# Low halves of the prepared inputs on VectorE in place of GpSimd, with the scale folded in

## The chip, the core and the metric

The kernel runs on one core of a Trainium2 chip. A core has five engines that run side by side, each through its own instructions in a fixed order: TensorE (PE in the profile; its weight loads are PEld), VectorE (DVE), ScalarE (ACT), GpSimd (POOL) and SyncE (SP), which here only issues DMAs. An instruction waits for semaphores that others raise, and whatever is queued behind it on its engine waits too. The metric is device time of one execution in microseconds (us), lower is better. TensorE is granted one of two clocks, 1.2 or 2.4 GHz; the profile gives the granted clock as a share of the higher.

## What is computed

A recurrent attention layer (batch 4, 8 heads, 768 steps, head size 40), and two feed-forward layers on its output (3072 tokens, width 320, inner width 2048):

```python
for t in range(S):
    y[:, :, t] = np.einsum('bhd,bhde->bhe', rt, state)
    Sa = np.einsum('bhde,bhe->bhd', state, at)
    state_decay = state * wt[:, :, None, :] - np.einsum('bhd,bhe->bhde', Sa, bt)
    state = state_decay + np.einsum('bhd,bhe->bhde', vt, kt)
...
h = x @ w_in
g = h * (1.0 / (1.0 + np.exp(-h)))      # second layer: g = h - np.tanh(h)
return (g @ w_out).astype(np.float32)
```

## The kernel before

The 768 steps are cut into 12 chunks of 64 (c = 0 to 11). A chunk's inputs come in two halves of 16 heads (hf = 0 and 1), so there are 24 preparations; below they are counted n = 2c + hf, and "even" means hf = 0.

Float32 products are made of float16 matmuls: a value x is held as a high half, float16 of x, and a low half, float16 of x minus the high half, each multiplied apart. `prep(c, hf)` makes these halves. It takes four loaded tiles: `w` (decays), `ra` (a), `rkb` (k and b, 768 columns) and `rrv` (receptances r and values v, 384 columns each). VectorE scans the decays forward (L224) and backward (L230), scales a (L229) and k, b (L233). ScalarE rounds to float16 (L234 for k and b, L235 for a, L237 for r, L238 for v). GpSimd first multiplies r and v by 1024 in place (`pscale`, called on L236, shown under L193), and then makes the low halves: of k and b on L239 (on VectorE in chunk 0), of a, v and r by `psub`, which all stand under L190. High and low halves go to a tile `HL`, of which there is one, and from there twelve DMAs per preparation (L250) spread them over a tile `LR` (five buffers), which the matmuls read. While those DMAs read HL, the next preparation can't write it.

From LR, `p1` (L270, tile p1a) makes a chunk's 64x64 products, evicted by `p1e` (L278 mK on VectorE, L282 and L283 bP on ScalarE). `sol_in` transposes them (L305), and `sol_step` solves a triangular system on VectorE in 31 dependent steps of two instructions (L314 tmp, L316 Tl), which the other work of VectorE is put in between. `sol_out` transposes back (L326, L327). Merges (`mg`) and the chain `ch_x`, `ch_u`, `ch_s`, `ch_y`, `ch_m` follow on TensorE with evictions on ScalarE and VectorE; the state for the next chunk goes through `Md` (VectorE, L440), `MT` (ScalarE, L447) and its low half `lows` (GpSimd, L190). The first feed-forward layer (`hp` L569, `o` L591 to L593, with `gl` L579 on VectorE) runs on TensorE among this, about a chunk and a half behind. In the first 600 us all weights are also split into halves: `conv_f32` (L525 to L528 on ScalarE and VectorE), low halves by `psub` on GpSimd (tiles wih, woh, w2s). The second feed-forward layer runs alone after 862 us; there GpSimd makes only `gl`.

The order is not written by hand. Each task has a planned time from a table (`SC`); sorted by it they go to a scheduler, which places every instruction by a cost model of its own. A change of engine or length in `prep` so moves the order on all engines. `psub` and `pscale` are one line each: a `tensor_tensor` subtract and a `tensor_scalar` multiply on GpSimd.

Of the kernel before, what the change touches and what calls it, by code (L numbers as in the profile page):

```python
# [12 lines left out]
AF = mybir.ActivationFunctionType  # L13
ALU = mybir.AluOpType
# [4 lines left out]
C = 64  # L19
# [12 lines left out]
S_R = 2.0 ** 10  # L32
S_V = S_R
# [14 lines left out]
def _poly():  # L48
# [37 lines left out]
    x=(-0.9631, -0.0175, 2.3021, 1.3623),  # L86
# [20 lines left out]
def build(tc, pk, tv, w1i, w1o, w2i, w2o, out, nch=NCH, dbg=None):  # L107
    nc = tc.nc
    PE, ACT, DVE, POOL, SP = nc.tensor, nc.scalar, nc.vector, nc.gpsimd, nc.sync
# [67 lines left out]
    def planes(HL):  # L177
        return [HL[:, :, o:o + n] for o, n in ((0, LW), (LW, 2 * C), (RW, LW), (RW + LW, 2 * C))]
# [10 lines left out]
    def psub(out, a, b):  # L189
        POOL.tensor_tensor(out, a, b, ALU.subtract)  # L190

    def pscale(out, a, sc):
        POOL.tensor_scalar(out, a, sc, 0.0, ALU.mult, ALU.add)  # L193
# [16 lines left out]
    def prep(c, hf):  # L210
        w, ra, rkb, rrv = raw_t.pop((c, hf))
        hl = HL
        if c == 0 and hf == 1:
            hl = lr_slot().rearrange("p u n -> p (u n)")[0:120, 0:12 * RW].rearrange("p (j n) -> p j n", j=6)
            DVE.memset(planes(hl)[0][:, :, 3 * C:LW], 0.0)
        ll, rh, lh, rl = planes(hl)
        k0, v0 = (0, 2 * C) if c % 2 == 0 else (C, 0)

        av, kb, rv, vv = [x.rearrange("p (j t) -> p j t", j=6) for x in (ra, rkb, rrv[:, 0:384], rrv[:, 384:768])]

        pt = at_p.tile([120, 392], F32, tag="pq", name="pq", bufs=1)
        pr = at_p.tile([120, 392], F32, tag="pr", name="pr", bufs=1)
        pq = pt[:, 0:390].rearrange("p (j t) -> p j t", t=65)
        DVE.tensor_tensor_scan(pt[:, 0:390], w[:, 0:390], d1a.rearrange("p j t -> p (j t)"), 0.0, ALU.mult, ALU.add)  # L224
        DVE.reciprocal(out=d1b[:, 65:391:65], in_=pt[:, 64:390:65])
        DVE.tensor_scalar(lh[:, :, 3 * C:3 * C + 1], pq[:, :, C:C + 1], S_P * S_KB / P_INIT, None, ALU.mult)
        DVE.scalar_tensor_tensor(out=lh[:, :, 3 * C + 1:LW], in0=pq[:, :, C:C + 1], scalar=S_P * S_KB / P_INIT,
                                 in1=lh[:, :, 3 * C:3 * C + 1], op0=ALU.mult, op1=ALU.subtract)
        DVE.scalar_tensor_tensor(out=av, in0=av, scalar=-S_A * S_KB, in1=pq[:, :, 0:C], op0=ALU.mult, op1=ALU.mult)  # L229
        DVE.tensor_tensor_scan(pr[:, 2:391][:, ::-1], w[:, 2:391][:, ::-1], d1b[:, 2:391][:, ::-1], 0.0, ALU.mult, ALU.add)  # L230
        pi = pr[:, 2:392].rearrange("p (j t) -> p j t", t=65)[:, :, 0:C]
        kbv = kb.rearrange("p j (q t) -> p j q t", q=2)
        DVE.tensor_tensor(kbv, kbv, pi.unsqueeze(2).to_broadcast([120, 6, 2, C]), ALU.mult)  # L233
        ACT.activation(out=lh[:, :, k0:k0 + 2 * C], in_=kb, func=AF.Copy)  # L234
        ACT.activation(out=rh[:, :, 0:C], in_=av, func=AF.Copy)  # L235
        pscale(rrv, rrv, S_R)  # L236
        ACT.activation(out=rh[:, :, C:2 * C], in_=rv, func=AF.Copy)  # L237
        ACT.activation(out=lh[:, :, v0:v0 + C], in_=vv, func=AF.Copy)  # L238
        (DVE if c == 0 else POOL).tensor_tensor(ll[:, :, k0:k0 + 2 * C], kb, lh[:, :, k0:k0 + 2 * C], ALU.subtract)  # L239
        psub(rl[:, :, 0:C], av, rh[:, :, 0:C])  # L240
        psub(ll[:, :, v0:v0 + C], vv, lh[:, :, v0:v0 + C])
        psub(rl[:, :, C:2 * C], rv, rh[:, :, C:2 * C])
        if c == 0:
            gates["pool"] = nc.cur_bb.bb.instructions[-1]
        LR = lr_slot()
        for i in range(3):
            n = 6 if i < 2 else 4
            src, dst = hl[i * 40:i * 40 + 40, 0:n], LR[:, 6 * i:6 * i + n]
            for pl, s0, d0, w in ((0, RW, 0, LW), (0, LW, LW, 2 * C), (1, RW, 0, RW), (2, 0, 0, RW)):
                SP.dma_start(out=dst[pl * 40:pl * 40 + 40, :, d0:d0 + w], in_=src[:, :, s0:s0 + w])  # L250
        LR = LR[0:120].rearrange("p (u j) n -> p u j n", u=2)
        L, R = LR[:, :, :, 0:LW], LR[:, :, :, LW:RW]
        if c == 0:
            gates["sp"] = nc.cur_bb.bb.instructions[-1]

        for i, j0, n, u in ((0, 0, 6, 0), (1, 0, 2, 0), (1, 2, 4, 1), (2, 0, 4, 1)):
            h = 6 * i + j0 - 8 * u
            SP.dma_start(out=pd[c, hf, 40 * h:40 * (h + n), u].rearrange("(h d) t -> d h t", d=40),
                         in_=pq[40 * i:40 * i + 40, j0:j0 + n, 0:C])
        p63 = at_p.tile([40, 2, 8, 1], F32, tag="p63", name="p63", bufs=5)  # L260
        POOL.tensor_tensor(p63, L[0:40, :, :, 3 * C:3 * C + 1], L[0:40, :, :, 3 * C + 1:LW], ALU.add)
        L_t[c, hf], R_t[c, hf], P_t[c, hf] = L, R, p63
# [36 lines left out]
    def lr_slot():  # L299
        return at_p.tile([128, 16, RW], F16, tag="LR", name="LR", bufs=5)  # L300
# [356 lines left out]
    for c in range(nch):  # L657
        T0 = 8.0 * c
        T1 = T0 + (SC["d"][c] if c < len(SC["d"]) else 0)
        for hf in range(2):  # L660
            when(T1 + SC["raw"][hf], load_raw, c, hf, after=[("prep", c - 1 + hf, 1 - hf)] if c else [])
            when(T1 + SC["prep"][hf], prep, c, hf, after=[("load_raw", c, hf)] + ([("prep", c, 0)] if hf else []))
            when(T0 + SC["v"][hf], load_v, c, hf, after=[("ch_y", c - 1, 2 * hf), ("ch_y", c - 1, 2 * hf + 1)])
# [123 lines left out]
```

## Time and profile before

| | before |
|---|---|
| runs | 1231.36, 1231.57, 1233.86 us, median 1231.57 |
| profiled execution, its own time | 1226.61 us |
| its span, first to last instruction | 1224.9 us |
| mean granted TensorE clock | 0.951 |
| busy: PE, DVE, ACT, POOL | 85%, 77%, 67%, 33% of the span |

A busy share is a mean over stages: up to about 100 us TensorE has little to do, from 120 to 745 us attention, the first layer and the preparations run together, from 745 to 862 us the first layer finishes, and then the second runs alone. Rows of the trace name an engine, a line, the tiles written and read, the count, the busy time and the mean duration, and for waits what ended them. TensorE's waits are read as time lost, since its work stands in a fixed order and its backlog is there to be done.

### The profile page before, as it was taken

To read this page: it belongs to the slowest core of one execution; us is meant where nothing else is said; L and a number is where in the kernel's file an instruction comes from. 1 tells how busy PE (TensorE), PEld (TensorE's weight loads), DVE (VectorE), ACT (ScalarE), POOL (GpSimd) and SP (SyncE) were. 2 spreads that over 40 slices of the span, in tenths; PEclk is the share of its full clock that TensorE was granted. 3 is DMA by queue.
4 is the path that set the end of the run, shared out by engine and by line. 5 is a ranking of instruction groups with operands and counts; after the bars stand their busy time and mean duration, and the time that the engine had idled before them with its cause. 6 is when DMAs were issued, how large, how long until landed. Compare 5 with 4: busy or idle time off the path is not lost.

```text
span 1224.9 us, 32035 instructions
## 1 busy us (share of the span) xinstructions
PE 1035.7 (85%) x12624; PEld 861.4 (70%) x12624; DVE 943.0 (77%) x1847; ACT 819.7 (67%) x1586; POOL 402.9 (33%) x488
## 2 busy tenths in 40 slices
PE   0006659888989998988999999999899999999997
PEld 0006547777767777777778778888778888888885
DVE  6788899788877988888868887723367888888885
ACT  2468678756666576666655655544468888888885
POOL 5345352433323442343242321010033333333332
PEclk9998659989997999899999999999999999999998
DMA  6676655465645555464434332111711111111000
GB/s 161 180 195 180 176 157 148 142 160 139 162 114 153 138 140 159 128 176 127 123 105 118 106 80 73 31 37 25 224 27 25 25 36 25 25 25 31 18 12 23
DMA packets 187912, 126.35 MB, mean 103 GB/s; under 512 B 107696, under 2 KB 170224, under 8 KB 187760
## 3 DMA queue, kind: packets, MB, share of 16 engines
q1 hardware_dynamic: 187760, 124.29, 38.1%
q8 instruction: 99, 1.62, 0.6%
q14 instruction: 53, 0.43, 0.1%
HBM read 63.59 MB, written 17.83 MB: 66 GB/s over the span
## 4 chain that ended last, share of the span: by engine, by line
PE 27%; issue 18%; DMA 16%; DVE 13%; POOL 11%; ACT 8%; SPq 7%; POOLq 0%; DVEq 0%; ACTq 0%
PE hp L569 8%; POOL gl L190 6%; SPq L250 4%; DMA LR<-HL 3%; DMA w2d<-w2s 3%; PE o L593 3%; PE o L591 3%; PE o L592 3%; DVE Tl L316 2%; DVE tmp L314 2%; ACT cr L527 2%; PE psx L364 2%; POOL HL L190 2%; DMA rawrv<-pk 2%; PE mg L348 1%
## 5 line engine op out<-in xcount | busy, mean ns | idle before, releaser
L569 PE MATMUL hp<-xh,wih 128*128 128x256 f16 x960 | 189.6, 283 | 6.1 <-DVE gl L579 4.4
L569 PE MATMUL hp<-x,w 128*128 128x256 f16 x1344 | 189.3, 273 | 3.1 <-DMA x<-x2d 3.1
L190 POOL TENSOR_TENSOR gl<-q,gh 128x512 f16<-128x512 f32 x96 | 111.8, 1165 | 221.6 <-ACT gh L626 219.7
L569 PEld LDWEIGHTS <-w 128*128 128x128 f16 x1344 | 131.4, 98 | 26.0 <-DMA x<-x2d 3.6
L569 PEld LDWEIGHTS <-wih 128*128 128x128 f16 x1344 | 129.1, 101 | 27.7 <-issue 4.5
L316 DVE TENSOR_TENSOR Tl<-Tl,tmp 128x126 f32<-128x126 f32 (+22 forms) x372 | 122.4, 329 | 7.8
L314 DVE TENSOR_TENSOR tmp<-Al,Tl 128x126 f32<-128x126 f32 (+22 forms) x372 | 118.2, 318 | 10.3 <-ACT Al L306 3.1
L270 PE MATMUL p1a<-LR 120*128 120x64 f16 x384 | 28.7, 206 | 107.8 <-DMA LR<-HL 67.3
L591 PE MATMUL o<-woh,gh 128*128 128x320 f16 x384 | 116.4, 304 | 0.8 <-DVE x2o L602 0.4
L592 PE MATMUL o<-woh,gh 128*128 128x320 f16 x384 | 116.3, 303 | 0.0
L593 PE MATMUL o<-woh,gl 128*128 128x320 f16 x384 | 115.1, 303 | 0.5 <-DVE gl L579 0.5
L591 PE MATMUL o<-w,gh 128*128 128x320 f16 x384 | 112.3, 301 | 1.3 <-ACT gh L626 1.3
L592 PE MATMUL o<-w,gh 128*128 128x320 f16 x384 | 113.4, 301 | 0.0
L569 PE MATMUL hp<-xl,wih 128*128 128x256 f16 x384 | 108.8, 283 | 0.0
L593 PE MATMUL o<-w,gl 128*128 128x320 f16 x384 | 103.3, 301 | 0.5 <-POOL gl L190 0.5
L270 PEld LDWEIGHTS <-LR 120*128 120x128 f16 x384 | 21.2, 104 | 115.1 <-issue 67.2
L621 DVE SCALAR_TENSOR_TENSOR s<-s,z 128x512 f32<-128x512 f32 x96 | 71.4, 744 | 33.9 <-ACT s L619 32.9
L593 PEld LDWEIGHTS <-gl 128*128 128x128 f16 x768 | 75.8, 99 | 28.0 <-issue 1.7
L591 PEld LDWEIGHTS <-gh 128*128 128x128 f16 x768 | 75.8, 99 | 27.5 <-ACT gh L626 1.6
L592 PEld LDWEIGHTS <-gh 128*128 128x128 f16 x768 | 75.8, 99 | 26.0 <-issue 0.8
L579 DVE SCALAR_TENSOR_TENSOR gl<-hp,gh 128x512 f16<-128x512 f32 x96 | 65.5, 683 | 34.5 <-ACT gh L578 34.0
L625 DVE COPY_PREDICATED q<-mk,t 128x512 f32<-128x512 int32 x96 | 79.1, 824 | 9.4
(145 smaller groups left out, 2855.3 us busy)
## 6 DMA issues: line engine op xcount, KB each, us to landing
LR<-HL SPq DMA_DIRECT2D x92, 150.9 KB
rawkb<-pk SPq DMA_DIRECT2D x23, 360.0 KB
rawrv<-pk SPq DMA_DIRECT2D x23, 360.0 KB
cr<-w1i SPq DMA_DIRECT2D x16, 384.0 KB
cr<-w2i SPq DMA_DIRECT2D x16, 384.0 KB
cr<-w1o SPq DMA_DIRECT2D x16, 320.0 KB
cr<-w2o SPq DMA_DIRECT2D x16, 320.0 KB
w2d<-w2s SPq DMA_DIRECT2D x32, 160.0 KB
```

Of the source, the lines that this page charges most:

```text
L190: POOL.tensor_tensor(out, a, b, ALU.subtract)
L250: SP.dma_start(out=dst[pl * 40:pl * 40 + 40, :, d0:d0 + w], in_=src[:, :, s0:s0 + w])
L270: PE.matmul(pa[:, p, :], kb, R[:, u, p, 0:C], start=True, stop=True)
L314: DVE.tensor_tensor(tv_, Al[:, j + 1:, j:j + 1].to_broadcast([128, n, w]), Tl[:, j:j + 1, :w].to_broadcast([128, n, w]), ALU.mult)
L316: DVE.tensor_tensor(Tl[:, j + 1:, :w], Tl[:, j + 1:, :w], tv_, ALU.add)
L569: PE.matmul(o, wi[:, f, a], x[:, k], start=n == 0, stop=False)
L579: DVE.scalar_tensor_tensor(out=gl, in0=hp, scalar=S_G, in1=gh, op0=ALU.mult, op1=ALU.subtract)
L591: PE.matmul(o, gh[:, cs], wo[:, f, 0], start=f == 0, stop=False)
L592: PE.matmul(o, gh[:, cs], wo[:, f, 1], start=False, stop=False)
L593: PE.matmul(o, gl[:, cs], wo[:, f, 0], start=False, stop=f == NF - 1)
L621: DVE.scalar_tensor_tensor(out=s, in0=s, scalar=GAMMA, in1=z, op0=ALU.add, op1=ALU.mult)
L625: DVE.copy_predicated(q, mk.bitcast(I32), t)
```

## The change

GpSimd does nothing in a preparation any more but the small sum `p63`. The scale of 1024 for r and v is given to ScalarE's rounding and to the subtraction, which becomes a `scalar_tensor_tensor` on VectorE: x times the scale, minus the high half. `S_V` equals `S_R`. The tiles rkb, rrv and ra hold what they held, except that r and v are not overwritten.

```diff
         ACT.activation(out=rh[:, :, 0:C], in_=av, func=AF.Copy)
-        pscale(rrv, rrv, S_R)
-        ACT.activation(out=rh[:, :, C:2 * C], in_=rv, func=AF.Copy)
-        ACT.activation(out=lh[:, :, v0:v0 + C], in_=vv, func=AF.Copy)
-        (DVE if c == 0 else POOL).tensor_tensor(ll[:, :, k0:k0 + 2 * C], kb, lh[:, :, k0:k0 + 2 * C], ALU.subtract)
-        psub(rl[:, :, 0:C], av, rh[:, :, 0:C])
-        psub(ll[:, :, v0:v0 + C], vv, lh[:, :, v0:v0 + C])
-        psub(rl[:, :, C:2 * C], rv, rh[:, :, C:2 * C])
+        ACT.activation(out=rh[:, :, C:2 * C], in_=rv, func=AF.Copy, scale=S_R)
+        ACT.activation(out=lh[:, :, v0:v0 + C], in_=vv, func=AF.Copy, scale=S_V)
+        DVE.tensor_tensor(ll[:, :, k0:k0 + 2 * C], kb, lh[:, :, k0:k0 + 2 * C], ALU.subtract)
+        DVE.tensor_tensor(rl[:, :, 0:C], av, rh[:, :, 0:C], ALU.subtract)
+        for lo, x, hi, sc in ((ll[:, :, v0:v0 + C], vv, lh[:, :, v0:v0 + C], S_V), (rl[:, :, C:2 * C], rv, rh[:, :, C:2 * C], S_R)):
+            DVE.scalar_tensor_tensor(out=lo, in0=x, scalar=sc, in1=hi, op0=ALU.mult, op1=ALU.subtract)
```

The new low halves are on lines 238 (k and b), 239 (a) and 241 (v and r) of the changed kernel; every line behind them has a number lower by one.

GpSimd's rows before, at chunk 4's even preparation, beside the end of chunk 2 (the sum p63, the four low halves of HL, the low half of the state, the weights and the layer's input):

```order
L261 TENSOR_TENSOR p_3293<-LR 40x16
L239 TENSOR_TENSOR HL<-rawkb,HL 120x6x128
L190 TENSOR_TENSOR HL<-rawrv,HL 120x6x64
L190 TENSOR_TENSOR lows<-Md,MT 40x320
L190 TENSOR_TENSOR HL<-rawa,HL 120x6x64
L190 TENSOR_TENSOR HL<-rawrv,HL 120x6x64
L190 TENSOR_TENSOR w2s<-c_7288,w2s 128x320
L190 TENSOR_TENSOR xl<-pf,xh 128x3x128
L190 TENSOR_TENSOR lows<-Md,MT 40x320
```

The same place now:

```order
L190 TENSOR_TENSOR w2s<-c_7808,w2s 128x320
L190 TENSOR_TENSOR lows<-Md,MT 40x320 x2
L260 TENSOR_TENSOR p_3283<-LR 40x16
L190 TENSOR_TENSOR lows<-Md,MT 40x320
L306 MEMSET Tl 128x512
L190 TENSOR_TENSOR w2s<-c_7908,c_7915 128x128
L308 MEMSET Tl 64x16 x2
L190 TENSOR_TENSOR xl<-pf,xh 128x3x128
```

The rows of HL are gone, and the state's low half (lows) stands behind none of them.

VectorE's rows before, between chunk 3's `sol_out` and chunk 4's `sol_in` (L305):

```order
L227 SCALAR_TENSOR_TENSOR HL<-pq,HL 120x6
L224 SCALAR_TENSOR_TENSOR pq<-raww,d1a 120x390
L225 RECIPROCAL d1b<-pq 120x6
L229 SCALAR_TENSOR_TENSOR rawa<-rawa,pq 120x384
L230 SCALAR_TENSOR_TENSOR pr<-raww,d1b 120x389
L506 SCALAR_TENSOR_TENSOR pf<-psyt,pf 128x384
L579 SCALAR_TENSOR_TENSOR gl<-hp,gh 128x512
L440 SCALAR_TENSOR_TENSOR Md<-psm,p_1414 40x320
L278 TENSOR_TENSOR mK_118<-p1a,mask_k 64x512
L579 SCALAR_TENSOR_TENSOR gl<-hp,gh 128x512
L526 TENSOR_SCALAR cr<-cr 128x320
L305 STREAM_TRANSPOSE Al<-bP 64x1024
```

The same place now, up to two rows ahead of `sol_in` (L304 by the new numbers):

```order
L238 TENSOR_TENSOR HL<-rawkb,HL 120x6x128
L241 SCALAR_TENSOR_TENSOR HL<-rawrv,HL 120x6x64
L225 RECIPROCAL d1b<-pq 120x6
L229 SCALAR_TENSOR_TENSOR rawa<-rawa,pq 120x384
L239 TENSOR_TENSOR HL<-rawa,HL 120x6x64
L578 SCALAR_TENSOR_TENSOR gl<-hp,gh 128x512
L241 SCALAR_TENSOR_TENSOR HL<-rawrv,HL 120x6x64
L230 SCALAR_TENSOR_TENSOR pr<-raww,d1b 120x389
L525 TENSOR_SCALAR cr<-cr 128x384
L277 TENSOR_TENSOR mK_118<-p1a,mask_k 64x512
L578 SCALAR_TENSOR_TENSOR gl<-hp,gh 128x512
L505 SCALAR_TENSOR_TENSOR pf<-psyt,pf 128x384
```

The four low halves of the even preparation now stand ahead of `sol_in` on VectorE.

## Rows read from the trace of the kernel before

**Rows 1.** Page, busy times: engine, busy us, share of the span, instructions

```profile
PE 1035.7 (85%) x12624; PEld 861.4 (70%) x12624; DVE 943.0 (77%) x1847; ACT 819.7 (67%) x1586; POOL 402.9 (33%) x488
```

**Rows 2.** Windows: us, PE, PEld, DVE, ACT, POOL busy, clock, DMA, GB/s

```profile
38.00:98.00 60.00, 4.26 (x55) 3.30 (x56) 51.74 (x114) 37.04 (x69) 26.94 (x35) 1.00 0.73 199
120.00:745.00 625.00, 543.00 (x7772) 457.69 (x7771) 521.77 (x1144) 411.25 (x830) 222.07 (x286) 0.91 0.51 137
745.00:862.00 117.00, 117.00 (x1659) 99.42 (x1657) 55.65 (x123) 57.34 (x119) 11.29 (x16) 1.00 0.16 44
```

**Rows 3.** Waits of TensorE, 120 to 745 us: releaser, total us, times, longest

```profile
PE p1a L270 <- DMA LR<-HL: 15.3, 10, 4.7
PE mg L334 <- DVE W L326: 11.9, 2, 11.1
...
PE psu L379 <- DVE lows L390: 8.2, 5, 2.7
```

**Rows 4.** Page, the chain that ended last, shares of the span by line

```profile
PE hp L569 8%; POOL gl L190 6%; SPq L250 4%; DMA LR<-HL 3%; DMA w2d<-w2s 3%; PE o L593 3%; PE o L591 3%; PE o L592 3%; DVE Tl L316 2%; DVE tmp L314 2%; ACT cr L527 2%; PE psx L364 2%; POOL HL L190 2%; DMA rawrv<-pk 2%; PE mg L348 1%
```

**Rows 5.** Groups by form, GpSimd: count, busy us, mean ns, idle before

```profile
L190 POOL TENSOR_TENSOR gl<-q,gh 128x512 f16<-128x512 f32 x96 | 111.8, 1165 | 221.6 <-ACT gh L626 219.7 <-DVE t L624 1.8
L190 POOL TENSOR_TENSOR HL<-rawrv,HL 120x384 f16<-120x384 f32 x46 | 48.3, 1061 | 2.5 <-ACT HL L237 2.4
L239 POOL TENSOR_TENSOR HL<-rawkb,HL 120x768 f16<-120x768 f32 x22 | 38.3, 1742 | 27.0 <-ACT HL L234 10.1 <-DMA pd<-pq 8.5 <-DMA LR<-HL 3.3
...
L190 POOL TENSOR_TENSOR HL<-rawa,HL 120x384 f16<-120x384 f32 x23 | 22.3, 969 | 31.1 <-ACT HL L235 30.8
L193 POOL TENSOR_SCALAR rawrv<-rawrv 120x768 f32<-120x768 f32 x23 | 22.1, 959 | 63.3 <-DMA rawrv<-pk 56.5 <-DMA x2d<-x2o 3.4 <-DMA rawa<-pk 3.2
```

**Rows 6.** Timeline, odd preparation, 397.5 to 402 us: start, length

```profile
397.85 1.54 POOL L239 TENSOR_TENSOR HL<-rawkb,HL 120x768 f16<-120x768 f32 x1 [8.52 <-DMA pd<-pq]
399.35 0.91 POOL L190 TENSOR_TENSOR HL<-rawa,HL 120x384 f16<-120x384 f32 x1
...
398.00 1.55 DVE L316 TENSOR_TENSOR Tl<-Tl,tmp 128x126 f32<-128x126 f32 x1
399.58 0.83 DVE L314 TENSOR_TENSOR tmp<-Al,Tl 128x120 f32<-128x120 f32 x1
400.44 0.87 DVE L316 TENSOR_TENSOR Tl<-Tl,tmp 128x120 f32<-128x120 f32 x1
```

**Rows 7.** VectorE by line: page groups (mean ns), then ns shortest/median/longest

```profile
L316 DVE TENSOR_TENSOR Tl<-Tl,tmp 128x126 f32<-128x126 f32 (+22 forms) x372 | 122.4, 329 | 7.8
L314 DVE TENSOR_TENSOR tmp<-Al,Tl 128x126 f32<-128x126 f32 (+22 forms) x372 | 118.2, 318 | 10.3 <-ACT Al L306 3.1
...
L316 DVE TENSOR_TENSOR Tl<-Tl,tmp x372: 157/267/1578, 42.5 to 784.3; 128x126 f32<-128x126 f32 x18, 128x30 f32<-128x30 f32 x12, 128x56 f32<-128x56 f32 x12, 128x78 f32<-128x78 f32 x12
L314 DVE TENSOR_TENSOR tmp<-Al,Tl x372: 158/268/1616, 42.2 to 784.1; 128x126 f32<-128x126 f32 x18, 128x30 f32<-128x30 f32 x12, 128x56 f32<-128x56 f32 x12, 128x78 f32<-128x78 f32 x12
...
L229 DVE SCALAR_TENSOR_TENSOR rawa<-rawa,pq x23: 508/857/1696, 9.5 to 690.7; 120x384 f32<-120x384 f32 x23
...
L239 DVE TENSOR_TENSOR LR<-LR x1: 958/958/958, 22.7 to 22.7; 120x768 f16<-120x768 f32 x1
```

**Rows 8.** Timeline, even preparation, 298 to 311 us: start, length, idle before

```profile
299.07 0.84 ACT L234 ACTIVATE HL<-rawkb 120x768 f16<-120x768 f32 x1
...
300.05 1.54 POOL L239 TENSOR_TENSOR HL<-rawkb,HL 120x768 f16<-120x768 f32 x1 [2.74 <-ACT HL L234]
...
302.80 1.33 POOL L190 TENSOR_TENSOR lows<-Md,MT 40x320 f16<-40x320 f32 x1
...
305.04 0.86 POOL L190 TENSOR_TENSOR HL<-rawrv,HL 120x384 f16<-120x384 f32 x1
...
307.45 0.69 DVE L278 TENSOR_TENSOR mK<-p1a,mask_k 64x512 f32<-64x512 f32 x1 [2.33 <-PE p1a L270]
...
310.26 1.95 DVE L305 STREAM_TRANSPOSE Al<-bP 64x1024 f32<-64x1024 f32 x1 [1.16 <-ACT bP L283]
```

## The prediction

> **What bounds the kernel now.** I read the windows first. From 745 us on TensorE is busy all the time: in 745 to 862 us 117.00 of 117.00 us [rows 2]. Its work is a fixed sum and its backlog waits for it, so what can be won or lost lies before, where TensorE stands still: 625 - 543 = 82 us in 120 to 745 us, and ahead of that, as in 38 to 98 us, where VectorE with 51.74 of 60 us sets the pace and TensorE has 4.26 us of work [rows 2]. The change touches nothing behind the last preparation, whose L229 starts at 690.7 us [rows 7].
>
> Next the waits of TensorE in that stretch [rows 3]. The largest single cause is `p1a` waiting for the DMAs from HL to LR, 15.3 us in 10 waits; this is the end of a preparation. Two others are behind VectorE: the merge behind `sol_out`, 11.9 us, and `psu` behind lows, 8.2 us. So both the length of a preparation and the load of VectorE (521.77 of 625 us, 83%) [rows 2] reach TensorE. The chain that ended last passes through GpSimd's low halves for 2% of the span, about 24 us, and through the DMAs behind them, LR<-HL 3% and their issue 4% [rows 4].
>
> Last, how GpSimd and VectorE stand to each other [rows 6]. While GpSimd's subtraction of 1.54 us runs from 397.85, VectorE's `sol_step` of 128x126, whose group has a median of 267 ns [rows 7], takes from 398.00 to 399.55; the next two take 0.83 and 0.87 us beside GpSimd's next two. VectorE ends each step when GpSimd's ends. Work that GpSimd does "beside" VectorE is so partly paid by VectorE.
>
> **What the change removes.** On GpSimd 48.3 + 38.3 + 22.3 + 22.1 = 131 us [rows 5], with five more instructions in chunk 0. GpSimd is busy 402.9 us in all [rows 1], 111.8 of it gl in the second layer [rows 5]; it bounds nothing, and the removal is worth only what VectorE, the preparations and the state's low half waited for it.
>
> VectorE's regained time, bounded from both sides. Low: what `sol_step` and L229 take over their medians or shortest: 372 x (329 - 267) + 372 x (318 - 268) ns = 41.7 us, and 23 x (857 - 508) = 8.0 us [rows 7], together 50 us; moved work is 131 of the 291 us that GpSimd does outside gl, 45%, so 22 us. High: the odd preparation shown loses 1.55 + 0.83 + 0.87 - 3 x 0.27 = 2.4 us of VectorE [rows 6, 7]; were all 22 preparations behind chunk 0 like it, 53 us. Even ones run beside fewer steps of `sol`, so I take 40.
>
> The stage between ScalarE's rounding and the last low half gets shorter. In the even preparation shown ScalarE ends k and b at 299.07 + 0.84 = 299.91, and the last low half ends at 305.04 + 0.86 = 305.90: 6.0 us [rows 8], in which the state's low half also stands. GpSimd's last instruction is what the DMAs to LR wait for. This matters for the even preparations, because HL comes free only when the odd one ahead has left it.
>
> **What it adds.** On VectorE 72 subtractions of 384 columns and 22 of 768 (chunk 0 had two). No row has the first on VectorE; the nearest with the same size and two inputs from SBUF is L229, 508 ns at the shortest, 857 at the median [rows 7]; I take 0.53 us, since what lengthens L229 is the work that goes away. For the second there is one of 958 ns on VectorE [rows 7]. Sum: 72 x 0.53 + 22 x 0.96 = 38 + 21 = 59 us; with L229's median it would be 62 + 21 = 83. Net on VectorE: 59 - 40 = +19 us, bounds 59 - 53 = +6 and 83 - 22 = +61. The upper one counts as lasting a slowness that mostly leaves with its cause; I take +20 for the remainder of GpSimd's work in the way.
>
> ScalarE keeps its four roundings; a scale in them costs nothing (those with and without one have no rows that differ by it, and it has the slack of 411 of 625 us [rows 2]). DMAs stay the same in number and place. A new wait: VectorE now waits for ScalarE ahead of each low half, and `sol_in` stands behind it. In the even preparation shown VectorE idles 2.33 us and 1.16 us ahead of `sol_in` [rows 8], waiting for `p1a` and bP, so there the four new instructions (0.96 + 3 x 0.53 = 2.55 us) fit into 3.5 us of idle time. If this cover is gone, they delay `sol_in` by up to 2.55 us a chunk.
>
> **The sum.** The stage of 6.0 us becomes 2.55 us of VectorE plus some 1 us for the rows of other work between (the order has four ahead of the last low half), 3.5 us: each even preparation ends about 2.5 us earlier. The waits of `p1a` are 1.5 us on average, so most would vanish: I count 10 of the 15.3 us. Against it VectorE's +20 us over a stretch in which it idles 625 - 522 = 103 us and TensorE waits for it directly only in some of the 82 us: I charge a quarter, 5 us. From 38 to 98 us the new order gives VectorE ten more low halves between the first `sol_in` and `sol_out` (3 x 0.96 + 7 x 0.53 = 6.6 us), against three preparations' collisions at 2.4 us, 7.2 us: nothing. Sum: -10 + 5 = -5 us on the profiled execution's own 1226.6 us, 1221.6 us. The runs' median is 5.0 us above that, so the forecast is **1226.5 us**.
>
> The SBUF — State Buffer page of the Trainium skill (SBUF: two separate sides) says that VectorE, when it has two inputs from SBUF, and GpSimd share a pair of ports as an exclusive lock, held for the whole instruction. The trace agrees at the place shown, 1.55 us behind 1.54. If it held wherever the two run at once, the gain would be that of rival B.
>
> **The rivals.** *A, VectorE becomes the pace* (slower). `sol` is a chain of 62 dependent instructions on VectorE per chunk; the even low halves stand ahead of `sol_in`, the odd ones within it. If the idle time ahead of `sol_in` closes, because `p1a` also comes earlier, then all +20 us of VectorE lie on the path, and the 2.5 us gains are not used since the next chunk waits for `sol` anyway: up to 1231.6 + 20 = 1251 us, and about 1242 when half is hidden. It decides from the point where what a chunk adds exceeds the idle time there, 3.5 us at the place shown. For it: VectorE at 83%, and the merge's wait of 11.9 us behind `sol_out`. Against: TensorE, at 87% in the same stretch, has its own pace.
>
> *B, VectorE regains nearly all* (faster). The odd place lost 2.4 us in 3.3 us of GpSimd's work, 73%; of 131 us that is 95 us. Net VectorE 59 - 95 = -36 us; at the same quarter -9 us, with the -10 of the preparations -19: 1212 us. For it: L229's longest, 1696 ns. Against: the medians, by which most steps meet nothing.
>
> *C, nothing that counts* (same): the state's chain and the DMAs' issue set the pace; GpSimd's 131 us were hidden, and VectorE's idle 103 us takes the 20. 1231.6 us, within 2 us. That GpSimd's work stays where it is can be excluded: the new order has no row of HL on it.
>
> **How the numbers follow.** The forecast has 0.38 (1219 to 1229), B 0.10 (1207 to 1219), C 0.20, A 0.32 (1234 to 1251). Faster by over 0.2% (2.5 us, about what a measurement can tell from no change) is the forecast's most and B: 0.46; same: C and the forecast's edge, 0.22; slower 0.32. The range leaves out A's upper end and B's lower: 1213 to 1245. The forecast's own range is 1219 to 1229.
>
> **What would show it.** Right: `sol_step` (372 of each) falls from means of 329 and 318 ns to about 290; the new subtractions take 0.5 to 0.6 and 0.95 us; VectorE is busy some 20 us more before 862 us; waits of `p1a` for LR<-HL fall below 8 us; TensorE's 82 us of idle time fall by about 5. Wrong: the new subtractions wait in their turn for what GpSimd keeps and take over 0.8 us; `sol_in` comes later each chunk and the merge waits longer for `sol_out` (A); or TensorE's idle time moves to another stretch, since the scheduler has put every engine's rows anew, which no row of before can show.

## The result

Four runs of the changed kernel took 1247.91 to 1252.28 us, median 1250.49; the kernel before, beside it, 1231.81. The ratio is 1.0147, 95% interval [1.0123, 1.0171]: slower by 1.5%, where 1226.5 us was forecast, and above the range's upper end of 1245. The profiled execution has a span of 1250.0 us (1224.9 before) and a granted clock of 0.938 (0.951).

The page of the changed kernel, busy times (columns as in [rows 1]):

```profile
PE 1045.6 (84%) x12624; PEld 871.5 (70%) x12624; DVE 946.3 (76%) x1941; ACT 822.1 (66%) x1586; POOL 281.0 (22%) x370
```

GpSimd has lost 122 us. VectorE has 94 instructions more and yet only 3.3 us more of busy time, where +20 was forecast. So no heavier VectorE can explain the 25 us between the two profiled executions (the medians are 18.7 us apart; the profiled execution of the kernel before was 5 us under its median). TensorE is busy for 9.9 us more with the same 12624 matmuls, since its clock is lower (1035.7 x 0.951 = 985 and 1045.6 x 0.938 = 981), and stands still for 1250.0 - 1045.6 = 204.4 us, before 1224.9 - 1035.7 = 189.2: 15.2 us more. Those two make up the loss.

The groups of VectorE that answer to [rows 7] (line, tiles, count, busy us, mean ns, idle ahead of it), changed kernel:

```profile
L315 DVE TENSOR_TENSOR Tl<-Tl,tmp 128x126 f32<-128x126 f32 (+22 forms) x372 | 106.7, 287 | 7.8
L313 DVE TENSOR_TENSOR tmp<-Al,Tl 128x126 f32<-128x126 f32 (+22 forms) x372 | 106.4, 286 | 10.7 <-ACT Al L305 3.4
...
L241 DVE SCALAR_TENSOR_TENSOR HL<-rawrv,HL 120x384 f16<-120x384 f32 x46 | 26.2, 583 | 2.9 <-ACT HL L236 1.7 <-DMA LR<-LR 1.1
...
L238 DVE TENSOR_TENSOR HL<-rawkb,HL 120x768 f16<-120x768 f32 x23 | 21.8, 948 | 2.1 <-DMA LR<-HL 1.4 <-ACT HL L234 0.4
...
L229 DVE SCALAR_TENSOR_TENSOR rawa<-rawa,pq 120x384 f32<-120x384 f32 x23 | 13.0, 567 | 0.0
...
L239 DVE TENSOR_TENSOR HL<-rawa,HL 120x384 f16<-120x384 f32 x23 | 12.6, 547 | 3.5 <-ACT HL L235 3.5
```

All that the prediction said of single instructions holds: `sol_step` fell from 329 and 318 to 287 and 286 ns ("about 290"), the new subtractions take 547 to 583 and 948 ns ("0.5 to 0.6 and 0.95 us").

The windows that answer to [rows 2], and the waits of TensorE from 120 to 745 us that answer to [rows 3] (releaser, total us, times, longest), changed kernel:

```profile
38.00:98.00 60.00, 3.79 (x42) 2.66 (x42) 49.87 (x119) 35.55 (x64) 15.98 (x21) 1.00 0.78 199
120.00:745.00 625.00, 536.71 (x7490) 454.04 (x7488) 505.22 (x1183) 404.19 (x814) 124.01 (x188) 0.88 0.49 133
745.00:862.00 117.00, 115.43 (x1749) 98.94 (x1748) 71.14 (x166) 61.84 (x125) 12.14 (x20) 1.00 0.18 47
```

```profile
PE p1a L269 <- DMA LR<-HL: 25.0, 10, 8.5
PE mg L333 <- DVE W L325: 11.5, 4, 7.5
```

From 120 to 745 us VectorE works less than before (505.22 against 521.77 us) and TensorE does 282 matmuls fewer, at 0.88 of the clock instead of 0.91. The wait of `p1a` for the DMAs from HL to LR, which was to fall below 8 us, rose from 15.3 to 25.0 [rows 3]. Most of that is one place: three waits of 3.2, 7.3 and 8.5 us between 152 and 176 us. There TensorE in the kernel before waits 4.7 us for the same DMAs and then 11.1 us for the merge behind `sol_out`, so it loses 22.0 us (with 3.1 for `tmp`) where it lost 15.8.

That stretch and the rest, TensorE alone (stretch, its length, busy time and matmuls, clock, DMA share, GB/s), before, then the changed kernel:

```profile
120.00:180.00 60.00, 34.45 (x416) 0.56 0.63 163
180.00:745.00 565.00, 508.55 (x7358) 0.95 0.50 134
```

```profile
120.00:180.00 60.00, 29.09 (x394) 0.69 0.56 153
180.00:745.00 565.00, 507.62 (x7098) 0.90 0.49 131
```

TensorE stands still for 30.9 us instead of 25.5 from 120 to 180 us, and ahead of that for 102.6 instead of 96.7: 11 of the 15.2 us are lost before 180 us. From 180 to 745 us it stands still no longer than before (57.4 and 56.4 us), but does 260 matmuls fewer in the same busy time, at 0.90 of the clock instead of 0.95.

How far behind is read at `sol_in` (the row gives shortest/median/longest ns, then the first and the last start in us); before, then the changed kernel:

```profile
L305 DVE STREAM_TRANSPOSE Al<-bP x12: 1893/1923/1957, 38.6 to 752.3; 64x1024 f32<-64x1024 f32 x12
```

```profile
L304 DVE STREAM_TRANSPOSE Al<-bP x12: 1886/1912/1932, 40.4 to 777.0; 64x1024 f32<-64x1024 f32 x12
```

The last chunk's `sol_in` is 24.7 us late. A first part of it shows at once. VectorE from chunk 0's `sol_in` to its `sol_out` (stretch, its length, VectorE's busy time and instructions, clock, DMA share, GB/s), before and changed:

```profile
38.60:94.80 56.20, 47.94 (x113) 1.00 0.73 197
```

```profile
40.40:104.30 63.90, 51.82 (x131) 1.00 0.78 200
```

Ten low halves stand between the two that were not there before, but also the head of a fourth preparation (six instructions) and three more instructions of weight conversion, which the scheduler put there. That gave a first theory, called START below: the loss is made ahead of the first `sol_out`.

### The profile page after: what moved, and what is told of

Same layout as the page of the kernel before. It is cut to its first block, busy times and chain, and to the rows that moved or that the text cites. A ratio compares the mean times of both kernels' runs of the same rounds, so it can differ in the third digit from the quotient of the medians.

```text
span 1250.0 us, 31973 instructions
## 1 busy us (share of the span) xinstructions
PE 1045.6 (84%) x12624; PEld 871.5 (70%) x12624; DVE 946.3 (76%) x1941; ACT 822.1 (66%) x1586; POOL 281.0 (22%) x370
## 4 chain that ended last, share of the span: by engine, by line
PE 33%; issue 16%; DMA 15%; DVE 11%; SPq 9%; POOL 8%; ACT 7%; POOLq 0%; DVEq 0%; ACTq 0%
PE hp L568 10%; POOL gl L190 6%; SPq L249 5%; DMA LR<-HL 4%; PE o L592 3%; PE o L590 3%; PE o L591 3%; DMA w2d<-w2s 3%; PE psx L363 2%; PE psy L422 2%; DMA pd<-pq 2%; PE psu L378 2%; DVE tmp L313 1%; PE mg L347 1%; PE hp L569 1%
## 5 line engine op out<-in xcount | busy, mean ns | idle before, releaser
L568 PE MATMUL hp<-xh,wih 128*128 128x256 f16 x960 | 193.1, 288 | 2.9 <-ACT xh L506 2.7
L568 PEld LDWEIGHTS <-wih 128*128 128x128 f16 x1344 | 131.7, 103 | 27.4 <-issue 3.4
L313 DVE TENSOR_TENSOR tmp<-Al,Tl 128x126 f32<-128x126 f32 (+22 forms) x372 | 106.4, 286 | 10.7 <-ACT Al L305 3.4
L315 DVE TENSOR_TENSOR Tl<-Tl,tmp 128x126 f32<-128x126 f32 (+22 forms) x372 | 106.7, 287 | 7.8
L576 ACT ACTIVATE hp<-hp 128x512 f32<-128x512 f32 x96 | 56.6, 590 | 48.9 <-PE hp L569 44.6
```

Of the source, the lines that this page charges most:

```text
L313: DVE.tensor_tensor(tv_, Al[:, j + 1:, j:j + 1].to_broadcast([128, n, w]), Tl[:, j:j + 1, :w].to_broadcast([128, n, w]), ALU.mult)
L315: DVE.tensor_tensor(Tl[:, j + 1:, :w], Tl[:, j + 1:, :w], tv_, ALU.add)
L568: PE.matmul(o, wi[:, f, a], x[:, k], start=n == 0, stop=False)
L576: ACT.activation(out=hp, in_=hp, func=AF.Silu, scale=1.0 / (S_X * S_WI))
```

## The experiments

Two theories stood at the start. ORDER: the loss comes from the scheduler, which after the edit placed every engine's instructions anew. LOAD: it comes from the low halves on VectorE themselves and from ScalarE, which now waits for the raw r and v, wherever the rest stands.

To part them, a kernel is traced twice. The first program is only scheduled, and the order in which its instructions came out is read. The second gets that order by edges between neighbours on one engine, which are there to fix the order and add no wait. The trace of e18 bears the order out: up to 870 us the rows of VectorE and ScalarE that both programs have stand in it as in the kernel before. An edge joins only instructions that both programs have; low halves and scalings are left to the scheduler. `way(c, hf)` names the engine of k's and b's low half, that of a's, v's and r's, and whether the scale is folded. GpSimd's common instructions are held too.

```diff
+        for e, seq in order.items():
+            for p, q in zip(seq, seq[1:]):
+                tc.add_manual_dep(ins[e][q], ins[e][p].name, info, reason="order")
...
-    with tile.TileContext(nc, schedule_with_timeline_sim=True) as tc:
-        build(tc, ...)
+    _, order = program(order_of)
+    nc, _ = program(way, order)
```

"Old order" is that of the kernel before, "new order" that of the changed kernel.

### Engines and order, crossed (e1, e2, e18)

```diff
 def way(c, hf):
+    return ("DVE", "DVE", True)       # e1, e18;  e2: ("POOL", "POOL", False)
 def order_of(c, hf):
+    return ("POOL", "POOL", False)    # e1, e18;  e2: ("DVE", "DVE", True)
```

> The changed kernel's instructions (94 low halves on VectorE, scale folded), but on TensorE, ScalarE, SyncE and VectorE all instructions that both kernels have are held in the order of the kernel before; the low halves on VectorE stand where the scheduler then puts them. Theory ORDER (the scheduler's new order of every engine makes the loss, not the load on VectorE): the loss is gone, 1220 to 1233 us, ratio to before 0.990 to 1.001. Theory LOAD (the low halves on VectorE and ScalarE's wait for the raw r and v make the loss wherever the rest stands): 1244 to 1254 us, ratio 1.010 to 1.018. In between, 1234 to 1243, each has a part.

> The kernel before's instructions (low halves and scale on GpSimd), but on TensorE, ScalarE, SyncE and VectorE all instructions that both kernels have are held in the order of the changed kernel. Theory ORDER: this order costs by itself, 1244 to 1256 us, ratio to before 1.010 to 1.020. Theory LOAD: 1227 to 1236 us, ratio 0.997 to 1.003, since VectorE is as free as before.

> All low halves on VectorE in the old order, again, beside the two others: 0.994 to 0.998 by the first measurement.

| ratio to before | old order | new order |
|---|---|---|
| low halves on GpSimd | 1 | 1.0325 [1.0284, 1.0367] (e2, 1276.28 us beside 1236.08) |
| low halves on VectorE | 0.996 [0.9934, 0.9986] (e1, 1232.33 beside 1236.08), again 0.9953 [0.9929, 0.9977] (e18, 1225.68 beside 1232.28) | 1.0147 (the changed kernel) |

LOAD falls and ORDER stands, though e2 lost more than ORDER expected (1.010 to 1.020). Moving the low halves is a gain under either order, of 0.4% in the old one and of 1.7% in the new one; the new order costs 1.9% with the new engines and 3.2% with the old ones. In e2 the low halves on GpSimd stand in an order that was made for VectorE's, so its 3.2% and the 1.7% hold this misfit too. e1 and e18 are also the version that beats both kernels.

In e18 VectorE's busy time from the page, the window, the wait of `p1a` and `sol_in`:

```profile
PE 1037.1 (85%) x12624; PEld 862.7 (70%) x12624; DVE 944.8 (77%) x1941; ACT 819.1 (67%) x1586; POOL 281.2 (23%) x370
```

```profile
120.00:745.00 625.00, 542.06 (x7765) 458.21 (x7765) 522.53 (x1217) 409.84 (x828) 125.48 (x192) 0.91 0.51 137
```

```profile
PE p1a L293 <- DMA LR<-HL: 10.7, 6, 4.3
```

```profile
L328 DVE STREAM_TRANSPOSE Al<-bP x12: 1895/1932/1946, 38.3 to 752.3; 64x1024 f32<-64x1024 f32 x12
```

With the same low halves, VectorE, TensorE and the clock are back at their values of before, and the last `sol_in` starts at 752.3, as in the kernel before. In this order too the even preparation's four low halves stand ahead of `sol_in`, and they don't delay it: rival A said that they would. The trace can't show where the gain of 0.4% comes from, since this execution, with a span of 1226.5 us, is itself no shorter than that of the kernel before (1224.9).

### Which stretch of the order (e3, e4, e7, e8)

Low halves on VectorE in all four; one order up to a `sol_out`, the other behind it.

```diff
+    ahead = [p for _, p in first[:[mark for mark, _ in first].index(True) + 1]]
+    for e, n in ahead + [p for _, p in rest if p not in set(ahead)]:
+        by.setdefault(e, []).append(n)
```

> The changed kernel's instructions; everything that the kernel before has placed ahead of its first sol_out stands in its order, all the rest in the changed kernel's order, on every engine. With the old order throughout the ratio was 0.996, with the new one 1.015. Theory START (the loss is made ahead of the first sol_out, by more VectorE work between sol_in and sol_out of chunk 0, and carried to the end): 0.994 to 1.002, 1227 to 1237 us. Theory ALL ALONG (each stretch of the new order costs its own part: about 11 us ahead of the first sol_out, some 13 behind it): 1.004 to 1.009, 1239 to 1246 us. Theory LATER (sol of chunks 4 and 5 and the gap ahead of sol_in 3 make it all): 1.010 to 1.016.

> The reverse of the one before: the changed kernel's instructions in the new order up to the first sol_out, and then in the old order. Theory START: 1.011 to 1.016, 1247 to 1255 us. Theory ALL ALONG: 1.003 to 1.008, 1237 to 1245 us. Theory LATER: 0.994 to 1.001.

> The changed kernel's instructions in the new order up to the sol_out of chunk 3, in the old order from there, on every engine. Known: old throughout 0.996, new to the first sol_out then old 0.999, old to the first sol_out then new 1.014, new throughout 1.015. In the profile of the changed kernel sol_in of chunk 4 stands 19 us behind that of the new instructions in the old order, the end 20 us. Theory MIDDLE (the loss is made between the first sol_out and that of chunk 3, where the conversion of weights is densest): 1.008 to 1.014. Theory BEHIND (made from chunk 4 on): 0.998 to 1.004.

> The reverse: old order up to the sol_out of chunk 3, new order from there. Theory MIDDLE: 0.995 to 1.003. Theory BEHIND: 1.009 to 1.015.

Measured: e4 (new up to chunk 0's `sol_out`, then old) 0.9992 [0.9963, 1.002]; e7 (new up to chunk 3's, then old) 1.0065 [1.0036, 1.0095]; e3 (old, then new from chunk 0's) 1.0137 [1.0079, 1.0195]; e8 (old, then new from chunk 3's) 1.0124 [1.0074, 1.0175].

START is out: e4 keeps at most 0.3% of a first `sol` that is as long as in the changed kernel, and even that isn't clear of noise (the intervals of e4 and e1 overlap). e7 has 0.7% more than e4, and the changed kernel 0.8% more than e7. So the loss is made behind chunk 0's `sol_out`, on both sides of chunk 3's: e4 fits LATER, and e7 lies between BEHIND and MIDDLE. The sizes are rough: `sol_in` of chunk 3 starts at 240.4 us in e18, 259.1 in e7 and 260.8 in the changed kernel, and yet e7 ends early, so the old order behind the seam makes up for part of a delay that the new one keeps. e3 and e8 can't be read that way, since the seam itself costs: the new order behind a seam begins with what the old one had not yet done. In e3 VectorE (start, length, idle ahead of it and its releaser):

```profile
105.95 0.20 DVE L240 TENSOR_SCALAR HL<-pq 120x6 f16<-120x6 f32 x1 [5.24 <-DMA LR<-HL]
...
113.40 1.91 DVE L328 STREAM_TRANSPOSE Al<-bP 64x1024 f32<-64x1024 f32 x1
```

There `sol_in` of chunk 1 starts 21 us behind chunk 0's `sol_out` at 92.17; neither whole order has more than 6.7 us at this place. In e8 39 us lie between chunk 3's `sol_out` and chunk 4's `sol_in` (294.0 and 333.3 us), in the whole orders 11 to 18. These two runs are inconclusive.

### Is it the weight conversion that was drawn forward? (e9)

```diff
+HELD = ('conv_w1', 'conv_w2')
+        for n in order["EngineType.DVE"]:
+            what = kind.get(ins[n].name, (None, None))[0]
+            if what == "sol_step":
+                step = ins[n]
+            elif what in HELD and step is not None:
+                tc.add_manual_dep(ins[n], step.name, info, reason="held")
```

> The changed kernel as it is scheduled by itself, with one rule more: no instruction of a weight conversion on VectorE may stand ahead of the sol_step behind which it stood in the kernel before (the new order has 27, 29 and 24 of them in the first three sol, the old one 24, 26 and 23, and ends them at chunk 6 in place of 8). The rest of the order is the scheduler's and comes out new again. Theory CONVERSION (the loss comes from conversions drawn forward into the stretch where VectorE sets the pace): 0.994 to 1.003, 1229 to 1240 us. Theory WHOLE ORDER (the old order fits as a whole, and any other costs): 1.008 to 1.025.

Measured 1252.72 us beside 1236.88, 1.015 [1.009, 1.021]. The conversions are held back and the loss is as large as ever: the conversions drawn forward are not the cause. The head of the fourth preparation, which the new order draws forward too, was not tested apart.

### Does any edit cost an order? (e10, e11)

```diff
 def way(c, hf):
+    return ("DVE", "DVE", True) if c == 3 else ("POOL", "POOL", False)   # e10
...
+        if (c, hf) == (2, 0):                                             # e11
+            DVE.memset(lh[:, :, 3 * C:3 * C + 1], 0.0)
```

> The kernel before, with the change made in the two preparations of chunk 3 alone (8 of the 96 low halves, two scalings), and the scheduler's own order. Its direct effect is a twelfth of the 0.4% gained in the old order, below 1 us; but the scheduler's order differs from the old one on every engine from chunk 2 on. Theory WHOLE ORDER (the old order fits better than what the scheduler makes after any edit): 1.005 to 1.030. Theory THIS ORDER (only what moving all low halves does to the order costs): 0.997 to 1.003.

> The kernel before with one instruction more: a memset of 120x6 on VectorE in the first preparation of chunk 2, whose result is overwritten by the next instructions; no work is moved. Its own price is far under 1 us, but the scheduler then orders all engines anew from there. Theory WHOLE ORDER (the old order fits better than what the scheduler makes after an arbitrary edit): 1.005 to 1.025, 1242 to 1266 us. Theory LOW HALVES (the new orders cost because of the subtractions that they have to place): 0.998 to 1.002.

e10 took 1249.99 us beside 1236.88, 1.0113 [1.0054, 1.0171]; e11 1239.38 beside 1232.54, 1.0044 [1.0014, 1.0074], just under what was expected of it. Eight of 96 low halves moved cost nearly as much as all of them (the intervals overlap), and a single memset costs 0.4%, about 5 us. The memset itself in e11's trace:

```profile
L227 DVE MEMSET HL<- 120x6 f16 x1 | 0.1, 63 | 0.0
```

In e10 the waits of TensorE from 120 to 745 us begin with

```profile
PE p1a L293 <- DMA LR<-HL: 26.5, 10, 8.6
```

which is the changed kernel's sign (25.0) without the changed kernel's work. So the old order is better than what the scheduler makes after each of the three edits (the change, e10, e11), and the new order of the changed kernel is no special case. Why the old order is the better one was not examined.

### Which engine's order (e14, e15)

```diff
     _, order = program(order_of)
+    order = {e: o for e, o in order.items() if e.split(".")[-1] in ['DVE']}   # e14
+    #  e15: ['PE', 'Activation', 'Pool', 'SP']
```

> The changed kernel's instructions; VectorE's alone are held in the old order (the low halves where the scheduler puts them between), the other engines' order is the scheduler's and comes out new. Theory VECTORE (its order decides, since it is the pace): 0.994 to 1.002. Theory OTHER ENGINES (the order in which TensorE, ScalarE and SyncE take their work decides): 1.008 to 1.025.

> The reverse: TensorE, ScalarE, GpSimd and SyncE in the old order, VectorE's order the scheduler's (the same conversions, preparations and low halves between each sol_in and sol_out as in the old order, but in other places among the steps). Theory VECTORE: 1.004 to 1.020. Theory OTHER ENGINES: 0.994 to 1.001.

e14 took 1286.6 us beside 1235.37, 1.0418 [1.0369, 1.0466]; e15 1256.62, 1.0168 [1.0128, 1.0208]. Both theories fall: e15 alone would fit VECTORE, but e14 contradicts it. Neither VectorE's order nor that of the others brings the old time back, and VectorE's old order with a new one of the rest is the slowest of all runs here. The first waits of TensorE from 120 to 745 us in e14:

```profile
PE p1a L293 <- ACT bP L306: 21.9, 3, 15.7
PE p1a L293 <- DMA LR<-HL: 16.5, 9, 3.7
```

and in e15:

```profile
PE mg L357 <- DVE W L349: 24.2, 5, 12.4
```

The last is VectorE ending `sol` late for a TensorE that wants the merge. The first is an eviction that ScalarE makes late. Before the longest of those three waits, 15.7 us that end at 402.8 us, ScalarE's rows in e14 are (start, length, idle ahead of it and its releaser):

```profile
395.76 0.52 ACT L249 ACTIVATE HL<-rawa 120x384 f16<-120x384 f32 x1 [8.19 <-DMA LR<-HL]
399.26 0.52 ACT L252 ACTIVATE HL<-rawrv 120x384 f16<-120x384 f32 x1 [2.98 <-DMA rawrv<-pk]
...
402.35 0.38 ACT L306 ACTIVATE bP<-p1a 32x256 f32<-32x256 f32 x1
```

ScalarE waits 8.2 us until the DMAs have left HL, then 3.0 us for r and v to arrive, and the eviction that TensorE needs stands behind both. So here one engine's queue holds up another that has work. That the whole loss is made in this way is argued; the numbers show only that no engine's order carries the gain alone.

### What a microsecond on VectorE costs (e6, e13)

e6 makes every low half twice, e13 adds 120 sums that nobody reads; both in the old order with the low halves on VectorE.

```diff
+            mine(lambda: E.tensor_tensor(ll[:, :, k0:k0 + 2 * C], kb, lh[:, :, k0:k0 + 2 * C], ALU.subtract))   # e6, each low half
...
+            for q in range(5):                                                                                  # e13
+                mine(lambda: DVE.tensor_tensor(pr[:, 2:386], pt[:, 0:384], pr[:, 2:386], ALU.add))
```

> As with the new instructions in the old order, but each low half on VectorE is made twice, the second time the same: 94 more instructions, about 58 us more on VectorE. If a quarter of VectorE's time reaches the end, as the prediction charged: +14 us on 1232, ratio 1.005 to 1.010. If VectorE's work is hidden in its idle time: 0.996 to 1.000. If VectorE is the pace of every chunk (rival A): +40 us and more, over 1.025.

> The new instructions in the old order, and at the end of each preparation five additions of 120x384 on VectorE whose result nobody reads, for which no DMA and no other engine waits: 120 of about 0.53 us, 64 us more on VectorE. With the low halves made twice (52 us more on VectorE, and each preparation longer) the time rose by 47 us over the low halves made once. If VectorE's own time is the pace: +45 to +60 us, ratio 1.033 to 1.045. If it was the longer way to the DMAs that cost there, and VectorE's time is mostly hidden: below +16 us, ratio under 1.010.

e6 took 1279.5 us beside 1237.04, 1.0361 [1.0314, 1.0408]; e13 1267.52 beside 1235.37, 1.0268 [1.0221, 1.0315]. VectorE's busy time on their pages:

```profile
PE 1042.7 (82%) x12624; PEld 866.1 (68%) x12624; DVE 996.1 (78%) x2037; ACT 820.5 (64%) x1586; POOL 301.6 (24%) x370
```

```profile
PE 1048.7 (83%) x12624; PEld 871.2 (69%) x12624; DVE 1000.4 (79%) x2061; ACT 821.0 (65%) x1586; POOL 300.3 (24%) x370
```

And on that of e1, with which they are compared:

```profile
PE 1041.7 (85%) x12624; PEld 866.8 (70%) x12624; DVE 944.4 (77%) x1941; ACT 819.3 (67%) x1586; POOL 282.7 (23%) x370
```

Against e1 (944.4 us busy and 0.996) e6 has 51.7 us more and is 4.0%, 50 us, longer: 0.96 us for each. e13 has 56.0 us more and is 3.1%, 38 us, longer: 0.68 us for each, below the 45 to 60 us expected. Load alone, for which nobody waits but VectorE's own queue, counts two thirds; where it also lengthens the preparations, nearly all. With the intervals of the ratios the two prices are 0.6 to 0.8 and 0.8 to 1.1. The quarter of the prediction is refuted.

### Which low halves make the gain (e5, e16, e17)

All in the old order. e5 leaves the scaling on GpSimd, e16 a's low half, e17 those of k, b and a.

```diff
 def way(c, hf):
+    return ("DVE", "DVE", False)      # e5;  e17: ("POOL", "DVE", True)
...
-        mine(lambda: E.tensor_tensor(rl[:, :, 0:C], av, rh[:, :, 0:C], ALU.subtract))
+        mine(lambda: POOL.tensor_tensor(rl[:, :, 0:C], av, rh[:, :, 0:C], ALU.subtract))   # e16
```

> Low halves on VectorE, but the scale of values and receptances stays on GpSimd (24 scalings of 1.84 us each, 44 us), all else in the old order. If the gain of 0.4% in the old order comes from GpSimd's shared port being free, about a third of it goes with these 44 of 131 us: ratio 0.996 to 0.999, and sol_step's mean between 285 and 320 ns, near 295. If it comes from the shorter preparation alone, which the scaling doesn't lengthen much: 0.994 to 0.997. If ScalarE's direct wait for the raw r and v costs, this is faster than with the scale folded, under 0.994.

> Old order; low halves of k and b, v and r on VectorE with the scale folded, that of a back on GpSimd. In the trace of the new engines in the old order a's low half costs VectorE 13.9 + 0.5 us; in the trace of before GpSimd's own cost VectorE some 6 us by collision. LEDGER: VectorE has 8 us less, at 0.6 to 0.9 that is 5 to 7 us: ratio 0.989 to 0.993 beside 0.996. WAY TO THE DMAS: GpSimd's subtraction (0.97 us beside 0.60) is not last in the row, so 0.994 to 0.998; if it becomes the last one that the DMAs wait for, 0.998 to 1.002.

> Old order; only the low halves of v and r on VectorE and the scale folded, those of k, b and a on GpSimd as in the kernel before. LEDGER: v, r and scale cost VectorE 30 us and give back some 24; k and b (22.9 against 17.5) and a (14 against 6) stay, so VectorE has 13 us less than with all moved: 8 to 12 us, ratio 0.986 to 0.990. WAY TO THE DMAS: GpSimd's 1.66 us for k and b stand in the way again, 0.995 to 1.000.

e5: 1238.13 us beside 1237.04, 1.0014 [0.9989, 1.0038]. The expectation took the scaling for 1.84 us and 44 us; it is 0.96 us and 22 [rows 5]. Yet leaving it on GpSimd takes the whole gain away. Its page has VectorE busy for 952.1 us, 7.7 more than e1, and 0.5% or 6.7 us are 0.87 of that, which fits the price above. But `p1a`'s wait for HL's DMAs is also back at 15.0 us (12.3 in e1), so the longer way to the DMAs would explain it as well. `sol_step` has means of 292 and 288 ns.

e16: 1226.23 us beside 1232.28, 0.9947 [0.9924, 0.9969]; e17: 1229.32, 0.9974 [0.9951, 0.9997]; e18 beside them 0.9953. LEDGER falls: e16's VectorE is busy for 938.5 us, 6.3 less than e18's, and the time is the same; e17 was to be the fastest and is not. Both lie where WAY TO THE DMAS had them. In e17 the wait of `p1a` and `sol_step`:

```profile
PE p1a L293 <- DMA LR<-HL: 16.8, 10, 4.4
```

```profile
L337 DVE TENSOR_TENSOR tmp<-Al,Tl 128x126 f32<-128x126 f32 (+22 forms) x372 | 115.8, 311 | 10.1 <-ACT Al L329 2.9
```

With k and b on GpSimd `p1a` waits as before (15.3), and `sol_step` takes 311 instead of 284 ns. `p1a`'s wait is 10.7, 11.7 and 12.3 us where the gain is 0.4 to 0.5% (e18, e16, e1), and 15.0 and 16.8 us where it is gone or smaller (e5, e17), while VectorE's busy time does not sort them. That points to the way to the DMAs, but it rests on one trace of each, and the intervals of e16, e17 and e18 overlap, so the shares are not settled, nor is where a should stand.

## Why the prediction was wrong

**The step that failed** is the one at its end: that the sum may be made in the order of the kernel before. The prediction says that TensorE's idle time may move "since the scheduler has put every engine's rows anew, which no row of before can show", and gives that neither a chance nor a price. It was the whole result: with the scheduler's own order there are 23 us on top (1.9%). With the order held, the change has the sign and the size that were forecast: the sum said -5 us, e1 and e18 measured 0.4% and 0.47% of some 1235 us, 5 to 6 us. The size is luck, since neither term of the sum, -10 and +5, came true, as the next three points show.

**VectorE regains.** Forecast 40 us, bounds 22 and 53; measured more. The groups of VectorE in e18 that fell:

```profile
L337 DVE TENSOR_TENSOR tmp<-Al,Tl 128x126 f32<-128x126 f32 (+22 forms) x372 | 105.6, 284 | 9.9 <-ACT Al L329 3.0
L339 DVE TENSOR_TENSOR Tl<-Tl,tmp 128x126 f32<-128x126 f32 (+22 forms) x372 | 103.9, 279 | 7.3
...
L243 DVE SCALAR_TENSOR_TENSOR rawa<-rawa,pq 120x384 f32<-120x384 f32 x23 | 14.1, 615 | 0.0
```

Against [rows 7], `sol_step` gave back 122.4 + 118.2 - 105.6 - 103.9 = 31.1 us and a's product 6.2; scans, conversions and the rest, which the prediction didn't count, gave another 17, some 54 in all. Added were 64 us (forecast 59). Durations so rose by 10 us in sum, and the page's busy time, which counts overlapping neighbours once, by 1.8. The forecast was +20. (The 131 us taken from GpSimd are such a sum too; its page lost 122. And chunk 0 gave up four more instructions, not five: GpSimd has 488 - 370 = 118 fewer, of which [rows 5] holds 114.)

**VectorE is charged a quarter.** Mis-sized: 0.68 to 0.96 us for each us (e13, e6). That VectorE has 103 us of idle time from 120 to 745 us did not mean that it could take 20 more. The two errors pull against each other: the forecast was 20 times a quarter, 5 us; 1.8 times 0.7 to 0.96 is 1 to 2 us.

**The stage of the even preparation, 6.0 to 3.5 us.** Not so. At the place of [rows 8], ScalarE's rounding of k and b and the four low halves in the changed kernel (start, length):

```profile
315.15 0.84 ACT L234 ACTIVATE HL<-rawkb 120x768 f16<-120x768 f32 x1 [1.16 <-DMA LR<-HL]
```

```profile
318.31 1.95 DVE L325 STREAM_TRANSPOSE W<-Al 32x1024 f32<-32x1024 f32 x1
320.18 1.88 DVE L326 STREAM_TRANSPOSE TT<-Al 64x1024 f32<-64x1024 f32 x1
322.08 0.96 DVE L238 TENSOR_TENSOR HL<-rawkb,HL 120x768 f16<-120x768 f32 x1
...
325.04 0.83 DVE L241 SCALAR_TENSOR_TENSOR HL<-rawrv,HL 120x384 f16<-120x384 f32 x1
```

From 315.15 + 0.84 = 315.99 to 325.04 + 0.83 = 325.87 it takes 9.9 us: VectorE stands in its queue ahead of them with `sol_out`'s transposes, 3.8 us, and with a good deal else. In e18 the same stage:

```profile
296.66 0.84 ACT L248 ACTIVATE HL<-rawkb 120x768 f16<-120x768 f32 x1
```

```profile
299.90 0.92 DVE L258 TENSOR_TENSOR HL<-rawkb,HL 120x768 f16<-120x768 f32 x1
...
303.40 0.55 DVE L263 SCALAR_TENSOR_TENSOR HL<-rawrv,HL 120x384 f16<-120x384 f32 x1
```

303.95 - 297.50 = 6.5 us, at this place no shorter than on GpSimd. "Some 1 us for the rows of other work between" was too little (the order printed ahead has three of them among the low halves, not four), and the first low half starts 2.4 us behind the rounding. `p1a`'s wait fell by 4.6 us in the old order (15.3 to 10.7; 12.3 in e1), not by 10, and it rose by 10 in the new one. TensorE's idle time from 120 to 745 us, which was to fall by 5, is 82.9 us in e18, before 82.0.

**The prologue counts nothing.** In the old order it gains: chunk 0's `sol` in e1 takes 53.0 us, with 45.36 us of VectorE in it,

```profile
38.90:91.90 53.00, 45.36 (x122) 1.00 0.77 211
```

against 56.20 and 47.94 before. In the new order it takes 63.9 us; but by e4 at most 0.3% reaches the end.

**The rivals.** A, VectorE becomes the pace, had 1234 to 1251 us, and the time fell into that span, but not by its mechanism: VectorE has 3 us more work, and with four low halves ahead of `sol_in` e18 is on time. Its price was right all the same (nearly 1 us for each, by e6); its load was not there. B's 95 us regained are far from the 54 measured, and its 1212 us are reached by no run. C is out: the changed kernel is slower by 1.5%, and in the old order the gain of 0.4% is measured twice.

## What to carry to other kernels

Where a scheduler orders the instructions, an edit has two prices, its own and that of the new order, and here the second was four times the first and of the other sign. Before giving up a change that "made it slower", hold the old order and measure again; the same goes for one that seems to have made it faster. GpSimd's work beside VectorE is partly paid for by VectorE: 131 us moved away gave it 54 us back, which almost paid for the 64 us of doing the work there.

## What the runs showed that was not expected

A wait that grows need not be the change's own: `p1a`'s for HL's DMAs is 25.0 us in the changed kernel and 26.5 in e10, where 8 of 96 low halves moved. TensorE's busy time isn't a constant of the work either: the same 12624 matmuls took 1035.7 us at a mean clock of 0.951 and 1067.3 at 0.923 (e14), and 9.9 us of the 25 in the changed kernel are of this kind. Why its clock is lower there isn't shown, and the amount of idle time doesn't decide it: from 600 to 745 us TensorE stands still for 9.1 us at 0.91, in the kernel before for 10.0 us at 0.98; and e6 stands still for 231.9 us in all at a mean clock of 0.945, the changed kernel for 204.4 at 0.938. And an idle engine is no cover: VectorE idles 103 of 625 us, yet sums that nobody reads cost two thirds of their time.
